# How many heads run in whole precision: ten or eight, in a kernel of attention with a memory and an FFN

## The chip, the core and the metric

The kernel runs on one core of a Trainium2 chip. Its engines work side by side, each on its own queue: PE (TensorE, the matmuls; PEld is its weight load), DVE (VectorE), ACT (ScalarE), POOL (GpSimd) and SP (SyncE, which here issues all DMAs). The metric is the device time of one execution in microseconds (us). It is taken several times and the median is given; the profile comes from one execution of its own.

## What is computed

Eight batches of eight heads, 576 rows of 64 columns each. A head mixes causal attention with a read from a memory matrix; the eight heads of a batch, side by side, are the rows of 512 that go into an FFN with a hidden width of 2048.

```python
scores = scale * np.matmul(q, k.transpose(0, 1, 3, 2))      # q, k, v: (8, 8, 576, 64), float32
scores = np.where(causal, -1000000000.0, scores)
a = softmax(scores)
local = np.matmul(a, v)
q_p = phi(q)                                                # elu(q) + 1
mem_out = (q_p @ M_prev) / (q_p @ z_prev + 1e-06)
x = g * mem_out + (1 - g) * local                           # g = sigmoid(beta), one per head
...
h = x @ w_in                                                # x: (4608, 512), w_in: (512, 2048)
out = (h * sigmoid(h)) @ w_out                              # w_out: (2048, 512)
```

## The kernel before

Three streams of work are written as Python generators, and the loop at the end of the function (L590 to L611) takes steps from them in turn.

`attention` goes through the 64 heads. In iteration n it takes steps of `scores` for head n and, in between, steps of `values` for head n - 1. `scores` transposes k and q (L221), multiplies them in blocks of 128 rows (L250), takes the row's extreme with the mask on DVE (L252) and the exponential on ACT (L254); the last 64 rows are done as two halves side by side (L271 or L274, then L284 to L294). POOL scales each block by its reciprocal sum (L304). The end of `scores` makes phi(q) and its normalisation (L325 to L335). `values` transposes phi and the weights of the attention on PE (L351, L376 to L395), copies them out of PSUM and multiplies them with the memory matrix (L414) and v (L422) into one PSUM tile `x`, which goes to the tile `xt` of its batch.

`preparation` brings the 32 pieces of the FFN's weights into shape: SP loads a piece into `wraw` (L138), ACT, DVE and POOL turn its words into two float32r parts (L150 to L162), and the twelve pieces named in FLOW_IN and FLOW_OUT go back to memory and are fetched anew when they are used. PREP_RATE and PREP_AFTER, both 3.0, give out three pieces for nine steps of `attention`, so that the last pieces belong to the tenth head.

`ffn` works on units of 256 rows. It may begin when the eight heads of the first batch are done. Then it gets a share of 0.2, later 0.22 of its steps per step of attention, and what is left of it runs alone after the last head. Its matmuls are L552 and L532, its activation L563 to L569.

A head runs in one of two ways, told by the argument `whole`, which is `n < N_WHOLE` at L453 and L472:

- In whole precision the matmuls take float32 operands as they are. `scores` makes one copy of q (L224), and `values` copies out of PSUM once for each group (L356, L401, L403, L425). The operands have 64 rows for the scores and 64 columns for the values.
- In split operands each operand is a float32r number and a float32r rest, and both lie side by side in 128 rows or columns. `scores` makes them on ACT (L230, L231, L233, L237) and POOL (L232, L235), and multiplies twice for each block (L250 with `qq` and with `ql`). The last 64 rows go through L274, L275 and L277, and their copy through L307. POOL splits v and the memory matrix (L315 to L319). `values` splits on the way out of PSUM (L358 and L359, L406, L407 and L410), multiplies with both parts (L422 with `ph` and with `pl`), and adds two halves of `x` at the end (L429, L430).

Nothing of this order is final in the program text: `TileContext` at L632 lays the instructions out on each engine's queue by a model of their times, and puts in the waits. An engine works through its queue in the order thus given.

Of the kernel before, what the change touches and what calls it, by code (L numbers as in the profile page):

```python
# [25 lines left out]
NB = dict(vs=1, e=2, r=1, qp=1, ms=2, raw=1, qn=2, mr=3, zb=2, st=2, nrm=2, ph=2, pl=2, xb=1, tt=2)  # L26
PS_S, PS_T, PS_X, PS_H = 2, 2, 1, 1
FIRST_STEPS = 1
N_WHOLE = 10
ROW_BUFS = 4  # L30
W_AHEAD = 2
PREP_RATE = 3.0
# [8 lines left out]
def memory_attention_then_silu_ffn(ctx, tc, q, k, v, M_prev, z_prev, beta, w_in, w_out, out):  # L41
# [394 lines left out]
    def attention():  # L436
# [12 lines left out]
        for n in range(len(todo) + 1):  # L449

            first, made = iter(()), {}
            if n < len(todo):
                first = scores(*todo[n], raws.pop(0), rests.pop(0), made, n < N_WHOLE)  # L453
            one = two = True
# [11 lines left out]
            if n < len(todo):  # L466
# [3 lines left out]
                if h % 2 == 0:  # L470
                    xt[b, h // 2] = pool.tile([P, S], F32, tag=f"xt{h // 2}", name="xt", bufs=2)
                second = values(b, h, made, xt[b, h // 2], n < N_WHOLE)  # L472

# [162 lines left out]
```

## Time and profile before

| | us |
|---|---|
| median of 3 runs | 1314.09 |
| lowest, highest | 1312.9, 1319.24 |
| the profiled execution | 1315.66 |
| its span, first to last instruction | 1313.9 |
| PE busy in the span | 1266.3 (96%) |
| DVE busy | 898.1 (68%) |
| ACT busy | 884.5 (67%) |
| POOL busy | 822.9 (63%) |
| mean granted TensorE clock | 0.975 |

The busy time of an engine is the time in which at least one of its instructions runs by the trace; the ends of matmuls are modelled, so that a busy PE is not a PE at its peak. The granted clock is the share of full speed that the throttle lets TensorE have. A line of a group of instructions gives the source line, the engine, the operation, output and inputs, the shape, the count, busy time and mean duration, and after the second bar the idle time of the engine before these instructions with what ended it. A timeline gives start, duration, engine, line and what ran, with the idle time before it in brackets.

### The profile page before, as it was taken

How to read it: one execution, taken by the hardware profiler on the slowest of the kernel's cores; microseconds unless marked ns; L12 is line 12 of the kernel's file. 1: busy time of each engine (PE TensorE's matmuls, PEld its weight loads, DVE VectorE, ACT ScalarE, POOL GpSimd, SP SyncE). 2: the span in 40 equal slices, each digit the busy share in tenths (PEclk: the TensorE clock that was granted, in tenths of full speed). 3: DMA queues.
4: the chain of work that ended last, by engine and by line, in shares of the span. 5: the costliest groups of instructions: out<-in, count | busy, mean ns of one | idle time of the engine just before them, and what ended most of it. 6: DMA issues, size and time to landing. Idle time of an engine off the chain costs nothing.

```text
span 1313.9 us, 24653 instructions
## 1 busy us (share of the span) xinstructions
PE 1266.3 (96%) x7858; PEld 1084.0 (83%) x7858; DVE 898.1 (68%) x2472; ACT 884.5 (67%) x2143; POOL 822.9 (63%) x1133
## 2 busy tenths in 40 slices
PE   6988999999999999999999999999999999999998
PEld 2343458888999989998988989899898998999997
DVE  7988875778777777787767777777877775332222
ACT  6777866777787777777777777787878774322222
POOL 6878995777777777777777777767767763000000
PEclk9987779999999999999999999999999999999999
DMA  6766555555455555555555555555545432444444
GB/s 165 188 184 168 162 134 164 144 131 146 125 145 147 138 153 138 150 131 149 137 137 143 145 138 154 137 137 136 158 129 156 123 123 81 145 154 149 152 156 143
DMA packets 302994, 190.39 MB, mean 145 GB/s; under 512 B 258832, under 2 KB 267024, under 8 KB 302864
## 3 DMA queue, kind: packets, MB, share of 16 engines
q1 hardware_dynamic: 302864, 188.82, 51.9%
q8 instruction: 62, 1.02, 0.3%
q14 instruction: 68, 0.56, 0.1%
HBM read 173.02 MB, written 15.73 MB: 144 GB/s over the span
## 4 chain that ended last, share of the span: by engine, by line
PE 73%; DVE 11%; ACT 6%; issue 3%; POOL 3%; DMA 3%; SPq 1%; POOLq 0%; DVEq 0%; ACTq 0%
PE h L552 28%; PE acc L532 25%; PE x L422 7%; PE s L250 5%; PE tp L376 4%; PE tq L351 1%; PE x L414 1%; DVE s L252 1%; DVE wy L159 1%; DVE pl L407 1%; DVE st L290 1%; ACT p L254 1%; POOL p L304 1%; PE s L274 1%; DVE wy L154 1%
## 5 line engine op out<-in xcount | busy, mean ns | idle before, releaser
L552 PE MATMUL h<-xu,wi 128*128 128x256 f32 x2592 | 376.8, 287 | 8.7 <-DVE th L564 6.1
L552 PEld LDWEIGHTS h<-xu,wi 128*128 128x128 f32 x2592 | 343.0, 191 | 24.6 <-DVE th L564 7.8
L532 PE MATMUL acc<-wo,g 128*128 128x512 f32 x864 | 243.0, 398 | 0.0
L532 PE MATMUL acc<-flow,g 128*128 128x512 f32 x864 | 231.0, 394 | 0.5 <-DMA flow<-wo_s 0.5
L304 POOL TENSOR_SCALAR p<-p,st 128x384 f32<-128x384 f32 (+3 forms) x320 | 182.8, 592 | 75.3 <-DVE st L302 72.2
L564 DVE SCALAR_TENSOR_TENSOR th<-th,h 128x512 f32<-128x512 f32 x144 | 98.2, 683 | 143.5 <-ACT th L563 141.7
L532 PEld LDWEIGHTS acc<-flow,g 128*128 128x128 f32 x864 | 158.8, 188 | 33.6 <-DMA flow<-wo_s 1.0
L254 ACT ACTIVATE p<-s,st 128x128 f32<-128x128 f32 (+3 forms) x256 | 134.9, 528 | 69.9 <-DVE st L252 52.8
L569 POOL TENSOR_TENSOR g<-th,g 128x512 fp32r<-128x512 f32 x108 | 140.2, 1298 | 48.7 <-ACT g L567 46.9
L532 PEld LDWEIGHTS acc<-wo,g 128*128 128x128 f32 x864 | 149.1, 189 | 18.9 <-POOL p L304 0.5
L563 ACT ACTIVATE th<-h 128x512 f32<-128x512 f32 x144 | 85.9, 597 | 99.7 <-PE h L552 97.4
L407 DVE TENSOR_TENSOR pl<-tp,ph 128x384 fp32r<-128x384 f32 x216 | 118.5, 551 | 34.6 <-ACT ph L406 31.3
L252 DVE CUSTOM_DVE_ANT_0 s<-s,mask 128x128 f32<-128x128 f32 (+3 forms) x256 | 125.3, 491 | 23.1 <-PE s L250 19.6
L567 ACT CAST g<-th 128x512 fp32r<-128x512 f32 x144 | 89.2, 620 | 53.0 <-DVE th L564 52.1
L376 PE MATMUL tp<-ident,p 128*128 128x128 f32 x640 | 121.8, 291 | 3.2 <-POOL p L304 2.5
L552 PE MATMUL h<-xu,flow 128*128 128x256 f32 x864 | 122.6, 283 | 0.0
L406 ACT CAST ph<-tp 128x384 fp32r<-128x384 f32 x216 | 104.7, 490 | 26.1 <-PE x L422 21.2
L552 PEld LDWEIGHTS h<-xu,flow 128*128 128x128 f32 x864 | 112.8, 191 | 1.9 <-issue 0.3
L376 PEld LDWEIGHTS tp<-ident,p 128*128 128x128 f32 x640 | 82.2, 148 | 28.6 <-POOL p L304 9.0
L422 PE MATMUL x<-pl,vs 128*128 128x256 f32 x324 | 82.1, 308 | 0.9 <-DVE pl L407 0.9
L232 POOL TENSOR_TENSOR kk<-tt,kk 64x576 fp32r<-64x576 f32 x54 | 77.4, 1432 | 5.0 <-ACT kk L230 1.2
L422 PE MATMUL x<-ph,vs 128*128 128x320 f32 (+4 forms) x378 | 78.2, 275 | 1.4 <-POOL vs L316 0.8
(104 smaller groups left out, 2409.5 us busy)
## 6 DMA issues: line engine op xcount, KB each, us to landing
flow<-wo_s SPq DMA_DIRECT2D x144, 512.0 KB, 3.6
flow<-wi_s SPq DMA_DIRECT2D x72, 512.0 KB, 3.8
raw<-in_k SPq DMA_DIRECT2D x128, 72.0 KB, 2.5
raw<-in_q SPq DMA_DIRECT2D x128, 72.0 KB, 2.7
out<-o SPq DMA_DIRECT2D x36, 256.0 KB, 4.2
wraw<-in_moe_w_in SPq DMA_DIRECT2D x16, 512.0 KB, 4.4
qn<-in_q SPq DMA_DIRECT2D x64, 128.0 KB, 2.9
vr<-in_v SPq DMA_DIRECT2D x64, 128.0 KB, 2.5
```

The lines of the kernel that those rows point to most:

```text
L252: anchor["dve"] = nc.vector.tensor_tensor_reduce(s, s, mask[:, 3 * P - P * i:], QS, 3.0e38, ALU.add, ALU.min, st[:, i:i + 1]).ins
L254: nc.scalar.activation(pt, s, AF.Exp, bias=st[:, i:i + 1], scale=-1.0, accum_out=st[:, 10 + i:11 + i])
L304: nc.gpsimd.tensor_scalar(pb[x], pb[x], st[:, 15 + x:16 + x], 1.0, op0=ALU.mult, op1=ALU.mult)
L376: nc.tensor.transpose(t[:, o:o + P], pb[i][:, P * j:P * j + P], ident)
L406: nc.scalar.copy(ph[:, 0:o], t[:, 0:o])
L407: nc.vector.tensor_tensor(out=pl[:, 0:cut], in0=t[:, 0:cut], in1=f(ph[:, 0:cut]), op=ALU.subtract)
L422: nc.tensor.matmul(x[0:rows, q0:n], vs[0:n_k, j], part[0:n_k, o:o + n - q0], start=False, stop=last)
L532: nc.tensor.matmul(acc[t], ta, tb, start=p == 0 and c == 0 and n == 0, stop=p == NP - 1 and c == 1 and n == len(terms) - 1)
L552: nc.tensor.matmul(h[:, c], ta, tb, start=kk == 0 and n == 0, stop=kk == KD - 1 and n == len(terms) - 1)
L564: nc.vector.scalar_tensor_tensor(out=th, in0=th, scalar=1.0, in1=h, op0=ALU.add, op1=ALU.mult)
L567: nc.scalar.copy(hi, th)
L569: late.tensor_tensor(out=lo, in0=th, in1=f(hi), op=ALU.subtract)
```

## The change

One constant is changed. Heads are counted through the batches, so the heads numbered 8 and 9, the first two of the second batch, take the other way through `scores` and `values`; the first eight stay as they were, and 56 heads run in split operands and not 54.

```diff
 PS_S, PS_T, PS_X, PS_H = 2, 2, 1, 1
 FIRST_STEPS = 1
-N_WHOLE = 10
+N_WHOLE = 8
 ROW_BUFS = 4
 W_AHEAD = 2
 PREP_RATE = 3.0
```

Both ways have the same number of steps, so the turns in which the three streams are written out do not change.

## The prediction

> **What bounds the kernel now.** I read the 40 slices of the page first, for the granted TensorE clock, and then the table of stretches (columns: length, then busy time and instruction count of PE, PEld, DVE, ACT and POOL, then clock, DMA share, GB/s). Heads 8 and 9 lie between 125 and 205 us: the last of the ten copies (L224) that only a whole head has starts at 142.8 us, and the last matmul of head 9's values at 193.28 us.
>
> ```profile
> PEclk9987779999999999999999999999999999999999
> ```
> ```profile
> L224 ACT COPY qf<-tt x10: 669/670/672, 6.5 to 142.8; 64x576 f32<-64x576 f32 x10
> ```
> ```profile
> 193.28 0.75 PE L422 MATMUL x<-ph,vr 128*64 128x320 f32 x2
> ```
> ```profile
> 125.00:205.40 80.40, 77.34 (x301) 44.10 (x301) 62.92 (x146) 60.78 (x148) 75.73 (x76) 0.75 0.60 162
> 205.40:330.00 124.60, 121.15 (x797) 107.80 (x796) 93.92 (x263) 91.13 (x228) 83.60 (x122) 1.00 0.53 141
> ```
> ```profile
> 157.00:172.70 15.70, 14.39 (x32) 5.79 (x32) 15.23 (x26) 11.26 (x27) 15.04 (x14) 0.50 0.43 108
> ...
> 330.00:1000.00 670.00, 661.16 (x4499) 609.20 (x4498) 503.55 (x1491) 511.14 (x1265) 491.78 (x719) 1.00 0.53 141
> ```
>
> From 205 us on the kernel is a TensorE kernel: from 330 to 1000 us PE is busy 661 of 670 us at clock 1.00, POOL only 492. Before that it is not. From 125 to 205.4 us the clock is 0.75 on average, PE is busy 77.3 of 80.4 us and POOL 75.7: both look full. In 157 to 172.7 us DVE, POOL and PE all fill over 14 of 15.7 us, at clock 0.50.
>
> A PE that is busy at half clock is not the same as a PE that is short of time, so I looked at the timeline of PE (start, duration, matmuls):
>
> ```profile
> 44.07 2.07 PE L250 MATMUL s<-tt,qf 64*128 64x512 f32 x2
> ```
> ```profile
> 166.99 2.07 PE L250 MATMUL s<-tt,qf 64*128 64x512 f32 x2
> ...
> 176.87 3.57 PE L552 MATMUL h<-xu,wi 128*128 128x256 f32 x15
> ```
>
> The 512-column score of a whole head took 2.07 us at 44 us, where the page prints clock 1.00, and the same 2.07 us at 167 us, where it prints 0.50: the slices before the first clock record say nothing, and all whole heads ran at the low clock. The second thing to see: the FFN comes in force only at 176.9 us. Until then nearly all that PE does is attention.
>
> What else ends waits there shows in the chain of waits taken over 125 to 206 us:
>
> ```profile
> by line: PE h L552 14.0%; PE x L422 13.3%; PE s L250 8.0%; PE tp L376 6.8%; PE acc L532 6.8%; DVE wy L159 6.1%; DMA wraw<-in_moe_w_out 5.3%; DMA wi_s<-flow 4.8%; PE x L414 4.6%; PE s L271 4.4%; issue 4.3%; DVE wy L154 4.2%; DVE s L252 2.7%;
> ```
>
> It passes through PE, through the weight preparation on DVE (L154, L159) and through DMAs. No single engine carries it, so I go by what each engine has left.
>
> **What comes off PE.** Heads 8 and 9 change from the first kind of row to the second (groups by line: busy, then mean ns):
>
> ```profile
> L422 PE MATMUL x<-pl,vs 128*128 128x256 f32 x324 | 82.1, 308 | 0.9 <-DVE pl L407 0.9
> L422 PE MATMUL x<-ph,vs 128*128 128x320 f32 (+4 forms) x378 | 78.2, 275 | 1.4 <-POOL vs L316 0.8 <-ACT ph L406 0.5
> ...
> L250 PE MATMUL s<-kk,qq 128*128 128x128 f32 x216 | 72.8, 340 | 4.1 <-ACT p L254 4.0
> L250 PE MATMUL s<-kk,ql 128*128 128x128 f32 x216 | 70.2, 325 | 0.0
> ...
> L422 PE MATMUL x<-ph,vr 128*64 128x320 f32 (+4 forms) x140 | 47.7, 473 | 1.5 <-ACT ph L401 1.5
> L250 PE MATMUL s<-tt,qf 64*128 64x128 f32 (+3 forms) x80 | 45.4, 684 | 13.9 <-ACT qf L224 7.2 <-DVE st L284 3.9 <-ACT p L254 2.7
> ...
> L414 PE MATMUL x<-qp,ms 128*128 128x256 f32 x108 | 34.5, 319 | 0.7 <-DVE xt L430 0.6
> L274 PE MATMUL s<-kk,qq 128*128 128x256 f32 x108 | 32.7, 318 | 0.2 <-ACT p L254 0.2
> ...
> L414 PE MATMUL x<-qp,mr 64*64 64x256 f32 (+1 forms) x40 | 18.5, 551 | 1.5 <-ACT xt L425 1.3 <-ACT qp L356 0.2
> L271 PE MATMUL s<-tt,qf 64*64 64x256 f32 (+1 forms) x40 | 18.4, 550 | 5.9 <-ACT p L254 3.3 <-DVE st L284 2.7
> ```
>
> Whole: 47.7 + 45.4 + 18.5 + 18.4 = 130.0 us over ten heads, 13.0 us a head. Split: 82.1 + 78.2 + 72.8 + 70.2 + 34.5 + 32.7 = 370.5 us over 54 heads, 6.9 us a head. The transposes are the same in both. So PE gives back 2 x 6.1 = 12.3 us.
>
> **What comes onto POOL, DVE and ACT.**
>
> ```profile
> L232 POOL TENSOR_TENSOR kk<-tt,kk 64x576 fp32r<-64x576 f32 x54 | 77.4, 1432 | 5.0 <-ACT kk L230 1.2
> ...
> L235 POOL TENSOR_TENSOR ql<-tt,qq 64x512 fp32r<-64x512 f32 x54 | 69.8, 1293 | 15.0 <-ACT qq L231 6.4 <-issue 4.1 <-POOL g L569 0.7
> ...
> L316 POOL TENSOR_TENSOR vs<-vr,vs 128x320 fp32r<-128x320 f32 x54 | 47.7, 883 | 3.6
> ...
> L315 POOL TENSOR_SCALAR vs<-vr 128x320 fp32r<-128x320 f32 x54 | 24.8, 460 | 14.3 <-PE x L422 11.7
> L319 POOL TENSOR_TENSOR ms<-mr,ms 128x64 fp32r<-128x64 f32 x54 | 18.7, 347 | 3.6
> ...
> L235 POOL TENSOR_TENSOR qq<-tt,qq 64x64 fp32r<-64x64 f32 x54 | 18.3, 338 | 1.4
> L277 POOL TENSOR_TENSOR pair<-pair,mask 64x64 f32<-64x64 f32 x54 | 18.0, 332 | 9.0 <-ACT pair L275 5.3
> L318 POOL TENSOR_SCALAR ms<-mr 128x64 fp32r<-128x64 f32 x54 | 13.6, 253 | 53.0 <-PE x L414 48.8 <-DMA raw<-in_q 1.8 <-DMA raw<-in_k 0.7
> L307 POOL COPY p<-p 64x64 f32<-64x64 f32 x54 | 13.5, 250 | 3.4
> ```
> ```profile
> L407 DVE TENSOR_TENSOR pl<-tp,ph 128x384 fp32r<-128x384 f32 x216 | 118.5, 551 | 34.6 <-ACT ph L406 31.3
> ...
> L359 DVE TENSOR_TENSOR qp<-tq,qp 64x384 fp32r<-64x384 f32 x108 | 52.8, 488 | 26.6 <-ACT qp L358 23.9
> L430 DVE TENSOR_TENSOR xt<-x,xb 64x256 f32<-64x256 f32 x108 | 49.0, 453 | 31.4 <-ACT xb L429 29.5
> ...
> L275 ACT COPY pair<-s 64x256 f32<-64x256 f32 x108 | 42.6, 394 | 7.3 <-PE s L274 4.7
> ...
> L233 ACT CAST qq<-tt 64x576 fp32r<-64x576 f32 x54 | 36.3, 672 | 1.3
> ```
>
> POOL: nine instructions a head, 1.432 + 1.293 + 0.883 + 0.460 + 0.347 + 0.338 + 0.332 + 0.253 + 0.250 = 5.59 us, for two heads **+11.2 us**. DVE: four L407, two L359, two L430, 4 x 0.551 + 2 x 0.488 + 2 x 0.453 = 4.09 us a head and a short L410 on top, 8.2 us for two. ACT: two more casts of L233's size and two L275, 2.1 us a head, 4.3 us. DMAs: none is added, removed or moved past another; SP's queue is the same.
>
> DVE has 80.4 - 62.9 = 17.5 us left in the stretch and ACT 19.6: both can take their part. POOL has 4.7 us left and cannot. So I expect POOL to set the end of this stretch, and PE's 12.3 us not to be seen in it.
>
> The added waits: PE's scores of heads 8 and 9 now wait for POOL's L232 and L235. They are issued one head ahead, and in the 54 split heads the row of L250 shows no idle time ended by POOL, so I cost that wait at nothing; if the cover went, PE's queue behind L250 (transposes and values of the head before) would wait up to one L232, 1.4 us a head. DVE's L284 now waits for POOL's L277, with the row maxima and the L294 exponential behind it. Both are in the forecast already, as they go at POOL's pace.
>
> **The sum.** How much of 11.2 us reaches the end? Two idle rows of POOL's timeline say (the bracket is the idle time before and its releaser):
>
> ```profile
> 150.22 1.33 POOL L156 TENSOR_TENSOR wy<-wy,wraw 128x512 uint32<-128x512 uint32 x1 [2.40 <-DVE st L299]
> ```
> ```profile
> 209.56 2.62 POOL L304 TENSOR_SCALAR p<-p,st 128x128 f32<-128x128 f32 x5 [4.15 <-DVE st L302]
> ...
> 214.05 1.29 POOL L569 TENSOR_TENSOR g<-th,g 128x512 fp32r<-128x512 f32 x1 [1.57 <-ACT g L567]
> ```
>
> Inside the stretch POOL idles 80.40 - 75.73 = 4.7 us, half of it at one place, behind a DVE instruction that is later too in the changed kernel. I let half be filled: -2.3 (ends: 0 and -4.7). At 205.4 us POOL idles 4.15 us for DVE's L302, which waits for scores: here POOL is ahead of PE, and a delay of POOL up to 4.15 us costs nothing: -4.15. After that PE is the bound and a delay that is left stays to the end. 11.2 - 2.3 - 4.15 = **+4.7 us**. Ends: +7.0 with nothing filled, +0.8 with all of it and the 1.57 us at 212 us too.
>
> The program's order is laid out anew from line 632's scheduler, for the later heads as well. The trace cannot show that; PE's idle time after 205 us, 3.5 us to 330 and 8.8 us to 1000, is what it could add to or take from, and I allow a third of it, about 4 us either way, as an estimate.
>
> The profiled execution took 1315.66 us with a span of 1313.9, 1.6 us over the median of 1314.09. By its own time the sum is 1320.4; on the median it is **1318.8 us**.
>
> **The rivals.** *PE was the bound (faster).* PE is busy 77.3 us of the stretch, more than POOL, and over half of the chain's listed shares are PE's. Then 12.3 us go: 1301.8 us. Against it: POOL's work does not fit in a shorter stretch. It needs that the scheduler puts weight preparation off past 205 us, where POOL is busy only 83.6 of 124.6 us; from about five postponed instructions of L156's 1.33 us on (11.2 less the 4.7 that POOL has) it decides. Chance 0.20.
>
> *DVE and POOL hold each other up (slower).* In the stretch their instructions lengthen when both run:
>
> ```profile
> 145.34 3.02 DVE L159 SCALAR_TENSOR_TENSOR wy<-wraw,wy 128x512 f32<-128x512 f32 x2
> ...
> 174.49 0.68 DVE L159 SCALAR_TENSOR_TENSOR wy<-wraw,wy 128x512 f32<-128x512 f32 x1
> ```
>
> The same L159 takes 1.51 us at 145 us and 0.68 us at 174 us. If the added 11.2 us of POOL lengthen, or lengthen DVE's work, by a third of that excess (a factor of 1.41 where L159 has 2.22), they cost 15.8 us, less the 4.15: +11.6, 1325.7 us. It decides once the added work costs over 10.7 us (6.6 and the 4.15). For it: the place is where DVE is fullest (15.2 of 15.7 us). Against: L407, L359 and L430 read a PSUM tile. Chance 0.28.
>
> The Trainium skill, "SBUF — State Buffer", section "Who interferes with whom", says that a VectorE instruction with two SBUF inputs contends with a GpSimd instruction that reads SBUF, and that issue order decides who is held. L159 has two SBUF inputs, and its 1.51 us against 0.68 agrees; by that rule the new POOL instructions, all readers of SBUF, would be paid a second time by DVE's preparation, which is this rival's 1325.7 us.
>
> *Nothing is seen.* POOL's delay is lost in slack and the FFN is as late as now: 1314. Chance 0.12.
>
> **How the numbers follow.** Forecast 0.40, rivals 0.20, 0.28 and 0.12. Half a per cent, 6.6 us, is about what a measurement of this kernel can tell from no change, so faster means below 1307.5 and slower above 1320.7. The forecast lies within but for 0.08 of its chance; the first rival is faster by 0.16 of its 0.20; the last has 0.02 on the faster side. Faster 0.18, same 0.46, slower 0.36. The range, 1304 to 1326, leaves about 0.08 at either end and takes in both ends of the sum with the 4 us of order.
>
> **What would show it.** Right: POOL stays over 90% busy in the stretch, which ends 4 to 9 us later; PE's busy time there falls by about 12 us; L232 comes 56 times. The first rival: the FFN's L552 starts well before 176.9 us and POOL's preparation reaches beyond 205 us. The second: L159 and L154 longer than now. Wrong altogether if the difference comes from after 330 us.

## The result, and the profile after

| | before | after |
|---|---|---|
| median, us | 1313.86 (1312.9 to 1319.24, 4 runs) | 1328.17 (1325.58 to 1331.37, 4 runs) |
| span of the profiled execution | 1313.9 | 1326.4 |
| mean granted clock | 0.975 | 0.97 |

The ratio is 1.0102, with an interval of 1.0067 to 1.0137: the change makes the kernel 14.3 us **slower**. The spans of the two profiles differ by 12.5 us, and that difference is what can be taken apart. Times are medians; one execution of `n8_warm6`, further down, took 5957 us and is in its median of 1329.66 us but not in its ratio, which compares undisturbed executions alone.

From the page of the changed kernel, the busy time of each engine and the group of splits of k:

```profile
PE 1260.1 (95%) x7848; PEld 1087.2 (82%) x7848; DVE 907.1 (68%) x2490; ACT 887.5 (67%) x2151; POOL 830.7 (63%) x1151
...
L232 POOL TENSOR_TENSOR kk<-tt,kk 64x576 fp32r<-64x576 f32 x56 | 80.4, 1435 | 4.9 <-ACT kk L230 0.8
```

The 56 splits are there. PE, the engine with by far the most work, has 6.2 us less of it (1266.3 before), and yet the kernel is longer. So PE must have lost time. What PE loses in a stretch is its length less busy time times clock: idle time, and the half of a half-clock time, together. I call it PE's shortfall. The table of stretches of the changed kernel (length, then busy time and count of PE, PEld, DVE, ACT, POOL, then clock, DMA share, GB/s):

```profile
125.00:205.40 80.40, 58.54 (x226) 35.25 (x226) 67.17 (x141) 55.60 (x134) 73.06 (x77) 0.75 0.54 142
170.00:210.00 40.00, 32.27 (x155) 24.54 (x155) 28.94 (x72) 26.39 (x65) 31.75 (x37) 0.76 0.52 150
210.00:320.00 110.00, 107.20 (x723) 97.94 (x722) 83.06 (x239) 82.43 (x204) 81.19 (x117) 1.00 0.52 140
320.00:480.00 160.00, 155.24 (x1035) 142.25 (x1034) 121.03 (x358) 119.03 (x300) 114.20 (x170) 0.98 0.52 140
480.00:1326.40 846.40, 833.01 (x5577) 763.88 (x5575) 531.57 (x1500) 538.73 (x1299) 459.26 (x677) 1.00 0.49 140
```

And the same stretches of the kernel before:

```profile
170.00:210.00 40.00, 39.62 (x198) 27.07 (x199) 24.77 (x69) 27.96 (x71) 33.82 (x41) 0.87 0.57 153
210.00:320.00 110.00, 108.13 (x724) 97.88 (x724) 83.42 (x232) 80.12 (x201) 75.89 (x109) 1.00 0.54 140
320.00:480.00 160.00, 156.54 (x1064) 143.69 (x1063) 122.34 (x357) 124.26 (x307) 118.61 (x175) 1.00 0.53 140
480.00:1313.90 833.90, 820.70 (x5495) 752.41 (x5493) 522.75 (x1479) 528.75 (x1275) 451.80 (x666) 1.00 0.49 140
```

| shortfall of PE, us | 170 to 210 | 210 to 320 | 320 to 480 | 480 to end | sum |
|---|---|---|---|---|---|
| before | 40 - 39.62 x 0.87 = 5.5 | 1.9 | 3.5 | 13.2 | 24.1 |
| after | 40 - 32.27 x 0.76 = 15.5 | 2.8 | 160 - 155.24 x 0.98 = 7.9 | 13.4 | 39.6 |
| difference | **+10.0** | +0.9 | **+4.4** | +0.2 | **+15.5** |

From 170 us on the changed kernel has 3.0 us less PE work left (busy time times clock, summed: 1116.9 against 1119.8), and 15.5 - 3.0 is the 12.5 us of the spans. So there are two losses, an early one of 10.0 us while heads 8 and 9 are under way, of which the 3.0 us of work already done are paid back, and a later one of 4.4 us between 320 and 480 us.

Three marks on the timelines give the delay as it stood there: the last word of the weight preparation, the first transpose of head 17, and that of the last head. Before:

```profile
195.25 1.30 POOL L162 TENSOR_TENSOR flow<-wy,flow 128x512 fp32r<-128x512 f32 x1
...
264.54 0.78 DVE L221 STREAM_TRANSPOSE tt<-raw 128x576 f32<-128x576 f32 x1
...
1032.90 0.78 DVE L221 STREAM_TRANSPOSE tt<-raw 128x576 f32<-128x576 f32 x1
```

After:

```profile
206.48 1.30 POOL L162 TENSOR_TENSOR flow<-wy,flow 128x512 fp32r<-128x512 f32 x1
...
270.88 0.77 DVE L221 STREAM_TRANSPOSE tt<-raw 128x576 f32<-128x576 f32 x1
...
1045.62 0.78 DVE L221 STREAM_TRANSPOSE tt<-raw 128x576 f32<-128x576 f32 x1
```

The preparation ends 11.2 us later, head 17 comes 6.3 us later, and the last head 12.7 us later.

**What PE waits for in the early loss.** PE's timeline of the changed kernel (start, duration; in brackets the idle time before and what ended it):

```profile
178.51 2.26 PE L552 MATMUL h<-xu,wi 128*128 128x256 f32 x15
...
185.72 0.56 PE L274 MATMUL s<-kk,qq 128*128 128x320 f32 x1 [2.26 <-ACT p L254]
...
189.95 2.90 PE L552 MATMUL h<-xu,wi 128*128 128x256 f32 x12 [3.67 <-DVE th L564]
```

L564 on DVE multiplies what ACT's L563 made, and frees the PSUM tile `h` for the next L552. ACT had its part ready before DVE took it up:

```profile
186.16 0.58 ACT L563 ACTIVATE th<-h 128x512 f32<-128x512 f32 x1
```

DVE's queue shows what stood ahead of L564:

```profile
186.37 1.41 DVE L154 SCALAR_TENSOR_TENSOR wy<-wraw,wy 128x512 uint32<-128x512 uint32 x2
187.81 0.15 DVE L289 COPY st<-st 64x1 f32<-64x1 f32 x1
187.99 1.22 DVE L152 TENSOR_SCALAR wy<-wraw 128x512 uint32<-128x512 uint32 x1
189.13 0.67 DVE L564 SCALAR_TENSOR_TENSOR th<-th,h 128x512 f32<-128x512 f32 x1
```

The input was there at 186.74 us; L564 began at 189.13, 2.39 us later, behind L154 and L152 of the weight preparation. An engine does its queue in order, so PE stood idle for 3.67 us. DVE is not the only queue in this chain: L563 reads what the matmuls at 178.51 us had finished by 180.77, and ACT began it at 186.16, after the work that stood ahead of it in its own queue. Of the 7.7 us that PE is idle between 170 and 210 us, 3.67 end with DVE's L564, and nearly all the rest with ACT (2.26 us at one place, before L274).

The twelve matmuls behind the 3.67 us took 2.90 us. In the kernel before, the same twelve on the same tiles ran at full clock:

```profile
184.75 1.68 PE L552 MATMUL h<-xu,wi 128*128 128x256 f32 x12
```

So the loss has two halves: idle time, at the place shown by a neighbour's place in an in-order queue, and half clock (the granted clock was 1.00 from 184 to 185 us and 0.50 from 186 to 196 us). POOL is not full meanwhile: 31.75 of 40 us.

### The profile page after: what moved, and what is told of

The parts are those of the page before. It is cut to its first block, busy times and chain, and to the rows that moved or that the text cites. A ratio compares the mean times of both kernels' runs of the same rounds, so it can differ in the third digit from the quotient of the medians.

```text
span 1326.4 us, 24676 instructions
## 1 busy us (share of the span) xinstructions
PE 1260.1 (95%) x7848; PEld 1087.2 (82%) x7848; DVE 907.1 (68%) x2490; ACT 887.5 (67%) x2151; POOL 830.7 (63%) x1151
## 4 chain that ended last, share of the span: by engine, by line
PE 71%; DVE 11%; ACT 8%; POOL 4%; issue 3%; DMA 2%; SPq 1%; POOLq 0%; DVEq 0%; ACTq 0%
PE h L552 27%; PE acc L532 24%; PE x L422 6%; PE s L250 5%; PE tp L376 4%; PE x L414 1%; PE tq L351 1%; POOL p L304 1%; DVE s L252 1%; DVE pl L407 1%; DVE tt L221 1%; DVE wy L152 1%; DVE st L290 1%; ACT p L254 1%; PE s L274 1%
## 5 line engine op out<-in xcount | busy, mean ns | idle before, releaser
L552 PE MATMUL h<-xu,wi 128*128 128x256 f32 x2592 | 376.3, 288 | 12.4 <-DVE th L564 8.8
L552 PEld LDWEIGHTS h<-xu,wi 128*128 128x128 f32 x2592 | 343.1, 191 | 28.8 <-DVE th L564 7.7
L304 POOL TENSOR_SCALAR p<-p,st 128x384 f32<-128x384 f32 (+3 forms) x320 | 179.4, 579 | 74.5 <-DVE st L302 74.0
L564 DVE SCALAR_TENSOR_TENSOR th<-th,h 128x512 f32<-128x512 f32 x144 | 98.2, 683 | 140.5 <-ACT th L563 138.6
L563 ACT ACTIVATE th<-h 128x512 f32<-128x512 f32 x144 | 86.0, 598 | 96.5 <-PE h L552 95.9
L407 DVE TENSOR_TENSOR pl<-tp,ph 128x384 fp32r<-128x384 f32 x224 | 123.1, 550 | 37.7 <-ACT ph L406 32.1
L406 ACT CAST ph<-tp 128x384 fp32r<-128x384 f32 x224 | 108.2, 489 | 30.4 <-PE x L422 25.4
L376 PE MATMUL tp<-ident,p 128*128 128x128 f32 x640 | 119.0, 288 | 7.9 <-POOL p L304 2.4
L552 PE MATMUL h<-xu,flow 128*128 128x256 f32 x864 | 124.1, 285 | 0.2 <-DMA flow<-wi_s 0.2
L552 PEld LDWEIGHTS h<-xu,flow 128*128 128x128 f32 x864 | 114.2, 192 | 2.1 <-DMA flow<-wi_s 0.4
L422 PE MATMUL x<-pl,vs 128*128 128x256 f32 x336 | 85.5, 309 | 1.0 <-DVE pl L407 0.9
L250 PE MATMUL s<-kk,qq 128*128 128x128 f32 x224 | 77.4, 348 | 7.1 <-ACT p L254 6.1
L232 POOL TENSOR_TENSOR kk<-tt,kk 64x576 fp32r<-64x576 f32 x56 | 80.4, 1435 | 4.9 <-ACT kk L230 0.8
```

The lines of the kernel that those rows point to most:

```text
L250: nc.tensor.matmul(s, ta[:, P * i:P * i + P], tb[:, 0:w], start=j == 0, stop=j == len(terms) - 1)
L304: nc.gpsimd.tensor_scalar(pb[x], pb[x], st[:, 15 + x:16 + x], 1.0, op0=ALU.mult, op1=ALU.mult)
L376: nc.tensor.transpose(t[:, o:o + P], pb[i][:, P * j:P * j + P], ident)
L406: nc.scalar.copy(ph[:, 0:o], t[:, 0:o])
L407: nc.vector.tensor_tensor(out=pl[:, 0:cut], in0=t[:, 0:cut], in1=f(ph[:, 0:cut]), op=ALU.subtract)
L422: nc.tensor.matmul(x[0:rows, q0:n], vs[0:n_k, j], part[0:n_k, o:o + n - q0], start=False, stop=last)
```

## The experiments

A shortfall below is always that of 170 to 210 us unless another stretch is named, by the sum above. It comes from one execution: the same order gave 5.5 us in the kernel before and 2.0 in `n10_rate`, 15.5 in the changed kernel and 13.9 in `n8_rate` (both described below), so that a difference of less than some 4 us is not told from none. Where a table gives the start of head 17, it is the first transpose of that head (L221), as above. A ratio is to the kernel before, on the same chip.

**One head, or the first two heads.** `n9` makes one head split and not two; `split_01` leaves 8 and 9 whole and makes 0 and 1 split.

```diff
-N_WHOLE = 10
+N_WHOLE = 9
```
```diff
-n < N_WHOLE
+2 <= n < N_WHOLE
```

> Only head 8 goes over to split operands. If the loss is the added work of splitting on POOL (5.6 us a head) and DVE while the weights are still being prepared, one head costs about half of two: 1319 to 1322 us, and the last L162 starts about 5.6 us later than the 195.3 us of the kernel before. If the loss comes from how the later heads are laid out, with PE idle and a low clock at 330 to 400 us, it need not lie between the two kernels at all: 1313 or 1328.

> Heads 0 and 1 are split and heads 2 to 9 are whole: eight whole heads as in the changed kernel, at another place, with the same added POOL and DVE work before the weights are ready. If work on POOL and DVE ahead of the last weight is the cause, the last L162 is late by up to 11.2 us, less what POOL has idle in the first 57 us (13 us by the stretches), so 1316 to 1322. If the place where the FFN begins (heads 8 and 9) is the cause, this kernel is at 1314 within 3 us.

`n9` took 1335.18 us (1.0139 [1.0109, 1.0170]) and `split_01` 1344.19 (1.0209 [1.0182, 1.0237]); both missed what was expected. But `n9` lost its time elsewhere: its head 17 is 0.6 us late, and the rest comes bit by bit to the end of the kernel. Its stretches:

```profile
170.00:210.00 40.00, 35.35 (x196) 26.16 (x195) 29.98 (x70) 27.51 (x68) 38.32 (x42) 0.93 0.51 138
...
480.00:1310.00 830.00, 813.97 (x5418) 745.93 (x5417) 525.69 (x1477) 524.70 (x1271) 453.40 (x668) 0.99 0.47 137
```

With one head split POOL is busy 38.32 of 40 us, far more than in the changed kernel, and the shortfall is 7.1 and not 15.5. In `split_01` the loss (22.8 us) is there by head 7, at some 106 us of the kernel before. So two split heads cost more there than at 8 and 9, and one alone costs nothing that can be told up to head 17.

**Which part of the work.** `one_part_89` runs heads 8 and 9 in the whole way with float32r operands in one part and leaves the rests out: PE's work falls, and all that is added is a copy on ACT and two casts on POOL for each head. On top of it `one_part_pool` makes POOL's rests, which nobody reads, `one_part_dve` DVE's, `one_part_both` both. `n8_dve_splits` is the changed kernel with POOL's subtractions of heads 8 and 9 on DVE.

```diff
+ONE_PART = (8, 9)
...
+            qq = pool.tile([P, S], F32R if one else F32, tag="kk", name="qf", bufs=QK_BUFS)
+            if one:
+                kr = qrow[h % QK_BUFS]
+                nc.scalar.copy(kr[0:64, 0:S], tt[0:64])
+                nc.gpsimd.tensor_tensor(out=qq[64:P], in0=tt[0:64], in1=f(kr[0:64, 0:S]), op=ALU.subtract)
...
+        kind = F32R if b * H + h in ONE_PART else kind
...
+                    if b * H + h in ONE_PART:
+                        pl = pool.tile([P, 512], F32R, tag="pl", name="pl", bufs=NB["pl"])
+                        nc.vector.tensor_tensor(out=pl[:, 0:cut], in0=t[:, 0:cut], in1=f(ph[:, 0:cut]), op=ALU.subtract)
...
```

(This is `one_part_both`; the others leave out the `nc.gpsimd` subtractions, the `nc.vector` ones, or both.)

```diff
-            nc.gpsimd.tensor_tensor(out=kk[64:P], in0=tt[0:64], in1=f(kk[0:64]), op=ALU.subtract)
+            eng = nc.vector if b * H + h in ON_DVE else nc.gpsimd
+            eng.tensor_tensor(out=kk[64:P], in0=tt[0:64], in1=f(kk[0:64]), op=ALU.subtract)
...
```

> Heads 8 and 9 take the whole way with float32r operands of one part only; the rests are left out, so the result of these two heads is coarser. PE gets even less work than with split operands, while POOL gets 0.7 us a head more and DVE nothing. If POOL's and DVE's splitting is what costs, this kernel is at 1314 or a few us below, 1308 to 1315. If PE was a bound of this stretch, it is 10 to 15 us faster than before, 1300 to 1304. If the loss comes with PE's relief itself (idle PE, low clock when the FFN begins), it is slower, 1320 to 1328.

> Heads 8 and 9 as in the one-part kernel (1312.5 us), and POOL also makes the rests of q, k, v and the memory matrix, which no matmul reads: 4.3 us more POOL work a head, nothing on DVE, ACT or PE. If POOL's added work sets the loss, this is 5 to 9 us over the one-part kernel, 1317 to 1322, with the last L162 late by about 8 us. If DVE's added work does, it is within 2 us of it.

> Heads 8 and 9 as in the one-part kernel (1312.5 us), and DVE also makes the rests of the transposed weights and of phi and adds once at the end, 4.1 us a head as in split operands; no matmul reads them. If POOL's added work sets the loss, this stays within 2 us of the one-part kernel. If DVE is the engine that is short, it is 4 to 8 us slower, 1317 to 1321.

> Heads 8 and 9 as in the one-part kernel (1312.5 us), with the idle work of both of the two kernels above. If the added work on POOL and DVE makes the whole loss, this comes near the changed kernel, 1322 to 1328. If the loss lies in what the split matmuls and their waits add, or in the order of the later heads, it does not: 1314 to 1320, or anything that fits neither of the two kernels above.

> The changed kernel with five of POOL's nine splitting instructions of heads 8 and 9 (L232, L235, L316, L319) on DVE: 4.3 us a head off POOL, about 3 us a head onto DVE. If POOL sets the loss, it is 4 to 9 us faster than the changed kernel, 1319 to 1324. If DVE does, it is slower, 1331 to 1335.

| | us | ratio | shortfall | head 17 |
|---|---|---|---|---|
| `one_part_89` | 1312.47 | 0.9975 [0.9958, 0.9993] | 40 - 38.08 x 0.91 = 5.3 | 260.74 |
| with POOL's rests | 1332.14 | 1.0131 [1.0096, 1.0167] | 40 - 32.21 x 0.75 = 15.8 | 277.06 |
| with DVE's rests | 1319.16 | 1.0032 [1.0015, 1.0049] | 40 - 37.59 x 0.87 = 7.3 | 261.26 |
| with both | 1334.05 | 1.0138 [1.0117, 1.0158] | 40 - 29.94 x 0.74 = 17.8 | 278.55 |
| `n8_dve_splits` | 1328.70 | 1.0092 [1.0064, 1.0120] | 40 - 32.73 x 0.83 = 12.8 | 270.54 |

The stretches of `one_part_89`, and then of `one_part_pool`:

```profile
170.00:210.00 40.00, 38.08 (x213) 28.57 (x213) 29.02 (x71) 29.14 (x75) 34.95 (x39) 0.91 0.52 158
```
```profile
125.00:205.40 80.40, 62.36 (x231) 35.17 (x232) 70.58 (x138) 57.08 (x140) 71.18 (x77) 0.68 0.51 139
170.00:210.00 40.00, 32.21 (x160) 22.94 (x159) 32.18 (x73) 30.68 (x78) 33.76 (x38) 0.75 0.48 132
```

Less PE work alone gains 0.25%, where PE as the bound would have given 12 us, 0.9%: the stretch wasn't bound by PE. POOL's subtractions alone, 4.4 us a head by their rows, bring the whole early loss: head 17 comes 16.3 us later than without them, more than the 8.8 us of work that they add, and the kernel is slower than the changed one (it and `one_part_both` lie above what was expected). (They also hold the buffers of k, v and the memory matrix longer, which wasn't told apart.) DVE's alone move head 17 by 0.5 us; that kernel's time lies in the range expected for DVE being short, but what it loses comes behind head 17. And yet POOL's busy time in `one_part_pool` is no fuller than before, 71.18 of 80.4 us. In `n8_dve_splits` POOL is relieved:

```profile
125.00:205.40 80.40, 60.13 (x254) 39.41 (x253) 66.99 (x140) 55.58 (x132) 63.67 (x65) 0.72 0.51 143
```

POOL is busy 9.4 us less than in the changed kernel (73.06), head 17 comes at the same time (270.54 and 270.88), and so does the end. It is neither faster, as expected if POOL were the limit, nor slower, as if DVE were. More POOL work costs, and less POOL work, with the same work on DVE, doesn't pay.

**Is it POOL's capacity?** The scaling L304 was moved from POOL to ACT, in the changed kernel for heads 8 and 9 (`n8_act_scale`), in the kernel before for heads 6 to 9 (`n10_act_scale`).

```diff
+            if b * H + h in ON_ACT:
+                nc.scalar.activation(pb[x], pb[x], AF.Copy, scale=st[:, 15 + x:16 + x])
+            else:
...
```

> The changed kernel with L304's scaling of heads 8 and 9 on ACT: 3.0 us a head off POOL, as much onto ACT, which has 20 us left between 125 and 205 us; nothing else changes. If POOL's queue is what holds PE at 170 to 210 us, the loss there falls from 15.5 us to 8 to 13 and the kernel is 3 to 7 us faster than the changed one, 1321 to 1325, give or take the 5 us that the layout of the later heads can move. If it is not POOL, the loss there stays at 15 us or grows.

> The kernel before with the same move for its heads 6 to 9, 12 us off POOL. If POOL sets the pace of the stretch before the FFN comes in force for whole heads too, head 12 begins 4 to 10 us earlier and the kernel comes to 1305 to 1312. If PE at half clock or DVE sets it, it stays at 1314 within 3 us, or is slower where ACT comes late: up to 1320.

`n8_act_scale` took 1327.06 us (1.0091 [1.0060, 1.0123]): nothing gained, and the shortfall stays at 15.5 us. `n10_act_scale` took 1327.75 (1.0107 [1.0085, 1.0129]). Its stretches, and the group of scalings on ACT:

```profile
125.00:160.00 35.00, 29.05 (x78) 13.49 (x78) 30.92 (x66) 28.40 (x69) 26.08 (x22) 0.60 0.61 174
160.00:205.40 45.40, 39.05 (x171) 24.55 (x169) 30.55 (x70) 34.73 (x86) 26.63 (x27) 0.82 0.55 146
```
```profile
L306 ACT ACTIVATE p<-p,st 128x384 f32<-128x384 f32 (+3 forms) x20 | 9.7, 561 | 4.1 <-DVE st L303 4.1
```

POOL is busy 26.08 + 26.63 = 52.7 us where the kernel before has 75.7, and the kernel is 12 us slower all the same, beyond what was expected. **With work taken off POOL the stretch is no shorter: POOL's capacity alone does not bound it.** The move has a price of its own: the row of ACT shows that the scaling waits 4.1 us for DVE's sums, now in ACT's queue, ahead of other exponentials. So this kernel doesn't show what POOL's work costs if nothing else changes.

**Beside the preparation or not.** Both kernels were given their weights earlier, so that the last piece is given out with the eighth head, and later.

```diff
-PREP_RATE = 3.0
-PREP_AFTER = 3.0
+PREP_RATE = 3.7
+PREP_AFTER = 3.7
```
```diff
-PREP_AFTER = 3.0
+PREP_AFTER = 2.0
```

> Ten whole heads, and the weights prepared at 3.7 pieces for nine steps and not 3.0, so that the last piece belongs to the eighth head. This is the other kernel of a pair and has no forecast that separates the theories by itself: 1310 to 1325 us.

> Eight whole heads with the weights prepared at 3.7 pieces for nine steps. If the loss is splitting work on top of preparation, it goes where the two no longer meet: this kernel is at most 4 us slower than its partner with ten whole heads, or faster. If the loss is in the splitting work itself or in the later order, it stays 10 us or more slower than its partner.

> Ten whole heads with the last three pieces put off in the same way. PE is full from 177 us on in the kernel before, so there is little for the FFN to gain: 1310 to 1316 us. If it loses more than 5 us, the loss lies after 210 us, in the order of the later heads.

> The changed kernel with the last three weight pieces put off by some four heads (about 8 us of POOL and 6 us of DVE work). If the loss is POOL's splitting on top of preparation while the FFN waits to begin, PE's idle and half-clock time between 170 and 210 us falls from 15.5 us to 6 to 9, and the kernel gains 5 to 9 us on the changed one as far as the late heads allow: 1319 to 1323 us. If POOL's place in the queue is not what holds PE there, it stays at 1326 or over.

| | ten whole heads | eight whole heads | difference | head 17, ten and eight | difference |
|---|---|---|---|---|---|
| as they were | 1313.86 | 1328.17 | +14.3 | 264.54, 270.88 | +6.3 |
| weights later | 1347.17 (1.0248 [1.0213, 1.0283]) | 1357.93 (1.0324 [1.0300, 1.0349]) | +10.8 | 260.98, 270.64 | +9.7 |
| weights earlier | 1330.56 (1.0118 [1.0097, 1.0139]) | 1329.11 (1.0110 [1.0091, 1.0129]) | -1.5 | 276.51, 277.26 | +0.7 |

With the weights given out faster, splitting heads 8 and 9 costs nothing that can be told, at head 17 or at the end. But that is not because the preparation is over. In `n8_prep_early` the first k of heads 8 and 9 is split (L232) while pieces are still being finished (L162):

```profile
147.36 1.74 POOL L232 TENSOR_TENSOR kk<-tt,kk 64x576 fp32r<-64x576 f32 x1
...
165.55 1.73 POOL L232 TENSOR_TENSOR kk<-tt,kk 64x576 fp32r<-64x576 f32 x1
...
193.51 1.51 POOL L162 TENSOR_TENSOR flow<-wy,flow 128x512 fp32r<-128x512 f32 x1
```

Seven of the 32 pieces are finished behind the first of these, where it is ten in the changed kernel. Nor is the loss between 170 and 210 us gone, as the stretches of `n10_prep_early` and then `n8_prep_early` show:

```profile
170.00:210.00 40.00, 39.03 (x169) 22.33 (x168) 23.17 (x69) 25.96 (x68) 26.95 (x38) 0.81 0.49 119
```
```profile
170.00:210.00 40.00, 30.54 (x148) 22.17 (x148) 30.68 (x68) 24.82 (x61) 32.50 (x39) 0.75 0.48 126
```

The shortfalls are 8.4 and 17.1 us. The kernel with split heads loses nearly as much more there as in the first pair. Ahead of that it is the other way round: between 125 and 170 us the shortfalls are 24.6 us with ten whole heads and 22.6 with eight, where the first pair has 17.1 and 21.5. So the pair shows only that the cost of split heads hangs on how the preparation is laid out around them, and not what they cost with no preparation beside them. The faster preparation itself costs as much at heads 0 to 7: 13.3 us by head 8 in `n10_prep_early`, whose time is outside what was expected.

Later weights do not help either: stretches of `n8_prep_late`, and then of `n10_prep_late`:

```profile
170.00:210.00 40.00, 38.52 (x220) 30.64 (x220) 22.48 (x64) 25.16 (x63) 24.95 (x34) 0.89 0.58 163
210.00:320.00 110.00, 98.23 (x596) 85.18 (x595) 84.83 (x233) 77.19 (x193) 81.95 (x114) 0.92 0.45 125
```
```profile
210.00:320.00 110.00, 98.82 (x619) 88.13 (x618) 84.98 (x225) 77.46 (x189) 79.86 (x109) 0.94 0.46 131
```

The shortfall of `n8_prep_late` is 5.7 us between 170 and 210 us, and 110 - 98.23 x 0.92 = 19.6 between 210 and 320. Its partner with ten whole heads has 110 - 98.82 x 0.94 = 17.1 in the second stretch, so that this loss belongs to the late weights, whatever the heads. The pair still differs by 9.7 us at head 17: the first 29 pieces are prepared where they were.

**The order of later heads.** The share of the FFN was changed by half a per cent of itself, in both kernels. Up to some 357 us all queues keep their order by it; behind that they are laid out anew, as they are by the change itself up to some 431 us.

```diff
-FFN_RATE = 0.22
+FFN_RATE = 0.221
```

> The kernel before with the FFN's later share at 0.221 and not 0.22, which changes nothing up to about 400 us and lays the later heads out anew. If the 4.3 us that the changed kernel loses at 320 to 480 us, and the larger late loss with nine whole heads, are accidents of that layout, this kernel too moves by 3 us or more to either side, with a low clock or idle PE after 320 us. If they come from the split heads themselves, it stays at 1314 within 2 us.

> The changed kernel with the same 0.221. The loss up to 210 us must be the same 10 us over the kernel before, as the order there is the same. If the late loss is an accident of layout, it differs from the changed kernel's by 2 us or more: 1320 to 1326, or 1331 and over.

`n10_rate` took 1322.0 us, 1.0061 [1.0039, 1.0084], and `n8_rate` 1333.85, 1.0145 [1.0117, 1.0173]. So a change with no work in it costs 0.6%, by order alone. Its head 17 comes 3.0 us early and its last head 5.8 us late; only 1.6 us of that are in the row below, and the rest comes bit by bit. The pair differs by 11.9 us, again near the 14.3, and by 7.5 us at head 17 (261.57 and 269.04). The stretches of `n10_rate`:

```profile
170.00:210.00 40.00, 39.16 (x216) 27.74 (x216) 26.45 (x68) 26.89 (x68) 34.88 (x44) 0.97 0.61 161
...
320.00:480.00 160.00, 154.91 (x1040) 140.57 (x1039) 123.39 (x353) 121.22 (x304) 116.53 (x169) 1.00 0.51 139
```

**Clock, or idle time?** In the changed kernel the score matmuls L250 of heads 8, 9 and 10 were issued 3 and 6 times more ahead of the real ones, which overwrite them, to fill PE's gaps.

```diff
+            for _ in range(6 if b * H + h in (8, 9, 10) else 0):
+                for j, (ta, tb) in enumerate(terms):
+                    nc.tensor.matmul(
+                        s, ta[:, P * i:P * i + P], tb[:, 0:w], start=j == 0, stop=j == len(terms) - 1)
```

> The changed kernel in which the score matmuls (L250) of heads 8, 9 and 10 are each done four times over, the first three for nothing: 7680 columns more a head, 3.2 us at full clock, where PE is idle anyway. If PE's half clock at 170 to 210 us is a cost of its own, the low time there falls from 19.2 us to under 10, and the loss from 15.5 to 9 to 12 although PE does more: 1322 to 1326 us. If the half clock only accompanies the idle time, the loss stays and the kernel is 0 to 5 us slower, 1328 to 1333.

> The same with six empty repeats, 6.4 us a head at full clock. If holding the clock up pays, the low time is shorter still and the time is near that of three repeats, 1322 to 1328; if not, 5 us or more slower than the changed kernel.

`n8_warm6` took 1329.66 us (1.0089 [1.0063, 1.0116]), the changed kernel's time, and `n8_warm3` 1337.75 (1.0159 [1.0134, 1.0184]). Stretches of `n8_warm6`, and then of `n8_warm3`:

```profile
125.00:205.40 80.40, 72.28 (x332) 52.40 (x332) 58.92 (x123) 53.49 (x126) 67.99 (x71) 0.78 0.50 135
170.00:210.00 40.00, 37.37 (x211) 31.14 (x211) 25.81 (x65) 25.74 (x60) 30.52 (x33) 0.87 0.47 134
320.00:480.00 160.00, 156.43 (x1063) 143.37 (x1061) 123.46 (x366) 122.90 (x308) 119.72 (x176) 1.00 0.52 143
```
```profile
320.00:480.00 160.00, 152.57 (x1001) 139.59 (x1000) 119.06 (x342) 116.22 (x290) 111.69 (x162) 0.97 0.50 135
```

Three repeats are free up to head 17: it begins at 270.43 us, and at 270.88 in the changed kernel. Six are not. PE is busy 72.3 us of the stretch and not 58.5, and head 17 comes at 278.87 us, 8 us later; the whole takes no longer only because this order loses nothing behind head 17, where the changed kernel loses 6.4 us. `n8_warm3` loses more there and misses what was expected by 5 us. The clock between 170 and 210 us goes up to 0.87 (and to 0.92 in `n8_warm3`) by work that is of no use, and nothing is gained by it. So in this kernel the low clock is no cost that could be had back by filling the idle time. Idle time is not all that sets the clock: in the kernel before it was 0.50 from 157 to 172.7 us, with PE busy 14.39 of 15.7 us.

Of the late loss the rows say more. The shortfall at 320 to 480 us is 3.5 us in the kernel before, 5.1 in `n10_rate` and 9.7 in `n10_act_scale`, all with ten whole heads; with eight it is 7.9 in the changed kernel, 3.6 in `n8_warm6`, 12.0 in `n8_warm3` and 12.4 in `n8_rate`. The two ranges overlap: the order alone can make a difference of this size. That the split heads have no part in it is not shown.

## Why the prediction was wrong, point by point

- **Where heads 8 and 9 lie.** The matmul at 193.28 us is the last of head 8's values; head 9's last is this one:

```profile
213.33 0.75 PE L422 MATMUL x<-ph,vr 128*64 128x320 f32 x2
```

So the stretch up to 205.4 us ends within head 9's values, and POOL's 4.15 us of idle time at 205.4 us were read there. Nor did all whole heads run at the low clock. The same scores took 1.11 us for head 9 and 0.64 for head 8:

```profile
154.09 0.64 PE L271 MATMUL s<-tt,qf 64*64 64x256 f32 x2
...
175.83 1.11 PE L271 MATMUL s<-tt,qf 64*64 64x256 f32 x2
```

Part of the 12.3 us that come off PE is therefore clock, and not work.

- **The bound.** That PE's 12.3 us would not be seen is right: `one_part_89` takes PE work away and gains 0.25%, `n8_warm3` adds some and head 17 is no later. The rival in which PE was the bound fell. That POOL sets the stretch, the reason given, is the step that failed first. POOL was to stay over 90% busy, and was busy 73.06 of 80.4 us (91%) over the stretch, but 31.75 of 40 us at its end; with 9.4 us less of POOL work (`n8_dve_splits`) head 17 came no earlier. What PE waited for between 170 and 210 us was DVE and ACT, and not POOL. Two busy shares near full were read as a limit.
- **The added POOL work, 11.2 us.** Its size is right: L232's mean is 1435 ns over the 56 heads, and the preparation ends 11.2 us later. That PE's busy time in the stretch falls by 12 us was too little: it fell by 18.8 (77.34 to 58.54), since the FFN's matmuls were late as well (226 matmuls in it and not 301).
- **Idle time filled, -2.3, and the lag of PE, -4.15.** The first term has the wrong sign: POOL's idle time in the stretch wasn't filled but grew, from 4.7 to 80.40 - 73.06 = 7.3 us. Behind the second stood the thought that PE is the bound from 205 us on and doesn't see a delay of up to 4.15 us. But PE stood idle for 40 - 32.27 = 7.7 us between 170 and 210 us, where it had 0.4, and the clock there fell from 0.87 to 0.76; the sum had both at nothing. That the early loss nevertheless came out within the ends of the sum (10.0 less the 3.0 us of PE work already done, 7.0; head 17 was 6.3 us late; the ends are 0.8 and 7.0) is luck: it was made of other terms.
- **The order of later heads, 4 us either way.** This term was mis-sized, and it takes the time past the range. Of the 12.5 us between the two profiles, 7.0 are early and 5.5 come behind 210 us, 4.4 of them between 320 and 480 us, where the two queues still differ. On the median of 1314.09 us the 12.5 give 1326.6, just over the upper end of 1326; the medians are 14.3 apart, as the profiled execution before was itself 1.6 us over the median. As an estimate from PE's idle time the 4 us were too small: half a per cent of FFN share moves the kernel by 0.6% with no work added.
- **DVE and POOL hold each other up.** Nearest by its time (1325.7), and its mechanism is in the rows, at nearly the size that it asked for. The preparation on DVE from 125 to 205.4 us, before and then after:

```profile
L159 DVE SCALAR_TENSOR_TENSOR wy<-wraw,wy 128x512 f32<-128x512 f32 x10 | 10.3, 1047 | 0.0
L154 DVE SCALAR_TENSOR_TENSOR wy<-wraw,wy 128x512 uint32<-128x512 uint32 x10 | 9.5, 947 | 0.1
L152 DVE TENSOR_SCALAR wy<-wraw 128x512 uint32<-128x512 uint32 x10 | 6.6, 656 | 0.1
```
```profile
L159 DVE SCALAR_TENSOR_TENSOR wy<-wraw,wy 128x512 f32<-128x512 f32 x11 | 10.4, 952 | 0.1
L154 DVE SCALAR_TENSOR_TENSOR wy<-wraw,wy 128x512 uint32<-128x512 uint32 x10 | 11.0, 1106 | 0.1
L152 DVE TENSOR_SCALAR wy<-wraw 128x512 uint32<-128x512 uint32 x10 | 9.9, 1000 | 0.1
```

L159 is 95 ns shorter, L154 159 ns and L152 344 ns longer: 4.1 us over ten of each, where the rival's lengthening is 15.8 - 11.2 = 4.6 us. The L152 that stood ahead of L564 at 187.99 us is one of the long ones, 1.22 us. But the lengthening does not go with the loss from kernel to kernel: in `one_part_both`, which loses most between 170 and 210 us, the three lines together are shorter than before (865 + 1142 + 518 against 1047 + 947 + 656 ns). So this rival is neither shown nor refuted. The rule of the Trainium skill, "SBUF — State Buffer", "Who interferes with whom", agrees with single instructions (1.51 against 0.68 us in the prediction's rows). What it costs this kernel as a whole stays open.

**What stands, and what stays open.** Shown: splitting heads 8 and 9 costs 14.3, 11.9 and 10.8 us in three pairs and nothing in the pair with the faster preparation, so that the early loss hangs on how split heads and preparation are laid out together; POOL's subtractions alone bring it, but not by filling POOL; and the order of later heads alone is worth 0.6%. Seen at one place: PE idle for 3.67 us, 2.39 of them behind a DVE queue in which the preparation stood ahead. That all of the early loss is of this kind, places in in-order queues, is argued from it and not shown; which place carries most of it stays open, since every kernel that changed something before 205 us moved all queues at once. Whether buffers held longer have a part wasn't tried apart: those of k, v and the memory matrix, and the four (`tag="row"`) in which the preparation's `wy` and the FFN's `th` take turns.

## What to carry to other kernels

An engine that is busy over 90% of a stretch isn't shown to be its bound until taking work off it makes the stretch shorter. Where several engines are that full, count what stands in whose in-order queue, and don't expect added work to cost its own length: 11.2 us of POOL work, with less PE work, came to 7.0 us up to 210 us, and 8.8 us of it in `one_part_pool` to 16.3 us at head 17. What two split heads cost hung on the work beside them: 11 to 14 us with the preparation as it was or with its end put off, nothing with a faster one, which made both kernels of the pair some 15 us slower than the kernel before. Where a scheduler lays the program out anew, find out first what a change with no work in it does to the time: here it was 0.6%.

## What the runs showed of the hardware

The half clock is not the same in two executions of one order: `n10_rate` and the kernel before have the same queues up to 357 us, and between 170 and 210 us one ran at 0.97 and the other at 0.87, by which (1 - clock, doubled, of 40 us) it was 2.4 and 10.4 us at half clock. Head 17 came 3.0 us earlier in the first, at 261.57 us:

```profile
261.57 0.78 DVE L221 STREAM_TRANSPOSE tt<-raw 128x576 f32<-128x576 f32 x1
```

In the changed kernel PE was idle for 2.26 us before L274 (to 185.72 us) and for 3.67 us before L552 (to 189.95 us). The granted clock was 1.00 from 184 to 185 us and 0.50 from 186 to 196 us, so that the half clock had begun before the longer wait did, and the twelve matmuls behind that wait took 2.90 us and not 1.68.

Of two instructions of DVE and POOL that run side by side, now the one is long and now the other. In the kernel before, the L159 of 0.68 us at 174.49 us ran beside a scaling L304 of 128x384 on POOL that took 1.27 us, where another one took 0.59; in the changed kernel an L152 that began at 184.71 us, 0.15 us behind POOL's L235, took 1.40 us, and the next, begun with POOL idle, 0.41.
